# Attention into a squared-ReLU feed-forward on one core: wider key chunks, the last one shared by two pairs of heads

## The chip, the core and the metric

The kernel runs on one core of one Trainium2 chip. A core has TensorE (matrix products, from weights that are loaded first, into PSUM), VectorE and ScalarE (element by element, from and to PSUM and SBUF), GpSimd, SyncE, and 16 DMA engines that all queues share. The engines run side by side, each through its own instructions in order, and wait for one another by semaphores. The metric is the time of one execution on the device in microseconds, the median of several runs. The profile is of one execution.

## The reference, cut to what matters

```python
# q, k, v: (8 batches, 12 heads, 448 positions, 64), fp32
scores = scale * np.matmul(q, k.transpose(0, 1, 3, 2))
m = np.max(scores, axis=-1, keepdims=True)
e = np.exp(scores - m)
attn = e / (np.sum(e, axis=-1, keepdims=True) + np.exp(-m) + 1e-09)
x = np.matmul(attn, v)            # heads side by side: (3584, 768)
h = x @ w_in                      # (768, 2048)
r = np.maximum(h, 0.0)
out = (r * r) @ w_out             # (2048, 768)
```

Without the subtraction of `m`, the weights are exp(s) / (sum of exp(s) + 1), and this is what the kernel computes.

## The kernel before

A *unit* is a pair of heads with a range of queries. Batch 0 has two rounds of six units (0 to 5 with queries 0 to 191, 6 to 11 with the other 256); every later batch has one round with all 448 queries, and units 12 to 17 are batch 1. The 448 keys of a head are cut into four chunks of 112, the keys with the same remainder by 4. A chunk's scores have its keys on the partitions and both heads' queries in the columns. ScalarE turns them into exps in `et`; the exps are the moving operand of `values`, and their sum over the chunks (`es`, made on VectorE) goes through a product with a constant column, which gives the row sums. In the batches 0 to 2, q and k are transposed on TensorE and copied by VectorE. The products with `w_in` (tiles in `ins`) and `w_out` (in `outs`) fill TensorE between the steps of the attention, in portions (`drain`, `rows`). A yield of a tile is one product; in the mode COLS2 each product is issued as two of 64 columns.

```python
RUN = 4
P = S // RUN            # 112
ON_PE = (0, 1, 2)
# ... pools: e_pool 4 buffers, es_pool 2, s_psum 2, x_psum 1, m_psum 3, v_pool 2 ...

def load_v(b, p0, p1):
    hs = slice(2 * p0, 2 * p1)
    if b not in vns:
        vns[b] = v_pool.tile([P, H, RUN, D], FP16, name="vn")
    nc.gpsimd.dma_start(out=vns[b][:, hs], in_=v_r[b, :, hs])

# ... load_natural: q by SyncE's and k by ScalarE's queue (pairs 0 to 2 of batch 0, fp32, into
# whole["q"] and whole["k"], two buffers of e_pool), the rest by GpSimd with a cast to fp16 ...

def transposes(b, pr):
    tp = mp_tile(FP16)
    for i, name in enumerate("qk"):
        for s in range(RUN):
            for h in range(2):
                nc.tensor.transpose(tp[64 * h:64 * h + 64, i, P * s:P * s + P],
                                    naturals[name, b, pr][:, h, s, :], ident[0:P, 0:P])
    if b not in qks:
        qks[b] = qk_pool.tile([128, 3, COLS], FP16, name="qk")
    parts = (0, S // 2, S) if b == 0 and pr < 3 else (0, S)
    for x, y in zip(parts, parts[1:]):
        nc.vector.tensor_copy(qks[b][:, 0:2, pr * S + x:pr * S + y], tp[:, :, x:y])

def scores(u, et, c, only=(0, 1)):
    b, pr, q0, n = u
    qk = qks[b]
    two = [] if n == S else s_psum.tile([P, 2, 512], FP32, name="sp")
    for kk in [2 * c + x for x in only]:
        sp = s_psum.tile([P, 2, 512], FP32, name="sp") if n == S else two
        if b in ON_PE:
            o = 0 if n == S else kk % 2 * n
            for h in range(2):
                r = slice(64 * h, 64 * h + 64)
                x = pr * S
                nc.tensor.matmul(sp[:, h, o:o + n], qk[r, 1, x + P * kk:x + P * kk + P],
                                 qk[r, 0, x + q0:x + q0 + n], start=True, stop=True)
        # ... batches 3 to 7, from transposed loads ...
        if n == S:
            exp(chunk(et, u, c, kk).rearrange("p (o x) -> p o x", o=2), sp[:, :, 0:S])
    if n < S:
        exp(et[:, 0:RUN * 2 * n].rearrange("p (c h x) -> p c h x", c=2, h=2)[:, c], two[:, :, 0:2 * n])

def add_chunks(u, et, es, half, step):
    n = u[3]
    if n == S:
        e = et.rearrange("p (k x) -> p k x", k=RUN)
        if step < 2:
            nc.vector.tensor_add((es, half[:, 0:2 * S])[step], e[:, 2 * step], e[:, 2 * step + 1])
        else:
            nc.vector.tensor_add(es, es, half[:, 0:2 * S])
    elif step == 1:
        nc.vector.tensor_add(half[:, 0:4 * n], et[:, 0:4 * n], et[:, 4 * n:8 * n])
    elif step == 2:
        f = half[:, 0:4 * n].rearrange("p (h j n) -> p h j n", h=2, j=2)
        nc.vector.tensor_add(es[:, 0:2 * n].rearrange("p (h n) -> p h n", h=2), f[:, :, 0, :], f[:, :, 1, :])

def values(u, et, xp, o=0):
    b, pr, _, n = u
    for kk in range(RUN):
        for h in range(2):
            nc.tensor.matmul(xp[64 * h:64 * h + 64, o:o + n], vns[b][:, 2 * pr + h, kk, :],
                             of_head(chunk(et, u, kk // 2, kk), u, h), start=(kk == 0), stop=(kk == RUN - 1))

def row_sums(us, sums):

    n = us[0][3]
    m = n * len(us)
    zp = mp_tile()
    for j, (u, parts) in enumerate(zip(us, sums)):
        for x, es in enumerate(parts):
            total = es[:, 0:2 * n]
            if n < S:
                total = total.rearrange("p (h n) -> p h n", h=2)
            for h in range(2):
                nc.tensor.matmul(zp[64 * h:64 * h + 64, j * n:(j + 1) * n], ones, of_head(total, u, h),
                                 start=(x == 0), stop=(x == len(parts) - 1))
    rcp = z_pool.tile([128, 512], FP32, name="rcp")
    nc.scalar.activation(out=rcp[:, 0:m], in_=zp[:, 0:m], func=AF.Ln, bias=one_b)
    nc.scalar.activation(out=rcp[:, 0:m], in_=rcp[:, 0:m], func=AF.Exp, scale=-1.0)
    return rcp

# ... front of the program ...
for pr in range(3):
    load_natural(0, pr, pr + 1)
nc.scalar.preload_act_table_set("natural_log_exp_and_others")
ident = consts.tile([128, 128], FP16)
make_identity(nc, ident)
load_v(0, 0, 3)
load_natural(0, 3, 4)
load_natural(0, 4, 6)
load_v(0, 3, 6)
for i in range(4):
    load_win(i, 8)
load_natural(1, 0, 3)
for i in range(4, 8):
    load_win(i, 8)
load_natural(1, 3, 6)
load_v(1, 0, 6)

FIRST = 192
units = [(0, pr, 0, FIRST) for pr in range(NPAIR)] + [(0, pr, FIRST, S - FIRST) for pr in range(NPAIR)]
units += [(b, pr, 0, S) for b in range(1, B) for pr in range(NPAIR)]
NU = len(units)

transpose_at = {pr - 1: [(0, pr)] for pr in range(1, NPAIR)}
for i, at in ((10, (1, 0)), (11, (1, 1)), (11, (1, 2)), (13, (1, 3)), (14, (1, 4)), (15, (1, 5)), (16, (2, 0)),
              (17, (2, 1)), (17, (2, 2))):
    transpose_at.setdefault(i, []).append(at)

# ...
keep_warm(9)
cast(0, 0)
transposes(0, 0)
keep_warm(1)
cast(0, 1)

for i in range(NPAIR):
    u, et, es, half = begin(i)
    mode[0] = COLS2
    scores(u, et, 0)
    if i < 2:
        scores(u, et, 1)
    if i in (3, 5):
        rcp = sums_of(i - 3)
    for at in transpose_at.get(i, ()):
        transposes(*at)
    if i == 0:
        cast(0, 2)
        keep_warm(1)
    if i:
        sums(i - 1)
    if i > 1:
        scores(u, et, 1)
    if i in (2, 4):
        xp = x_psum.tile([128, 512], FP32, name="xp")
    if i in (2, 3, 4):
        values_of(i - 2, xp)
    if i == 4:
        values_of(3, xp)
    if i in (3, 5):
        normalise(units[i - 3:i - 1], xp, rcp)
    if i in (1, 3, 5):
        keep_warm(1 + i // 5)

for i in range(NPAIR, 2 * NPAIR):
    u, et, es, half = begin(i)
    two = units[i - 2:i] if i % 2 == 0 else None
    if i % 2 or i == NPAIR:
        xp = x_psum.tile([128, 512], FP32, name="xp")
    mode[0] = COLS2
    scores(u, et, 0)
    if i == NPAIR:
        sums(i - 1)
        values_of(i - 2, xp)
        values_of(i - 1, xp)
        rcp = sums_of(i - 2)
        normalise(two, xp, rcp)
        scores(u, et, 1)
        queue(0, FIRST)
        share[0] = left() / (NPAIR + 4)
    else:
        for at in transpose_at.get(i, ()):
            transposes(*at)
        drain(16 * FIRST / 2.4 if i == NPAIR + 1 else share[0] * 0.45)
        scores(u, et, 1)
        values_of(i - 1, xp)
        if two:
            rcp = sums_of(i - 2)
        drain(share[0] * 0.3)
    add_chunks(u, et, es, half, 1)
    if two and i > NPAIR:
        normalise(two, xp, rcp)
    add_chunks(u, et, es, half, 2)
    if i > NPAIR:
        drain(share[0] * 0.25)
    if i == NPAIR + 5:
        load_natural(2, 0, 3)
        for n0 in (0, HALF):
            for j in range(2):
                load_wout(n0, j, 2)

for i in range(2 * NPAIR, 3 * NPAIR):
    u, et, es, half = begin(i)
    prev = units[i - 1]
    first = i == 2 * NPAIR
    if not first:
        xp = x_psum.tile([128, 512], FP32, name="xp")
    mode[0] = COLS2
    scores(u, et, 0)
    for at in transpose_at.get(i, ()):
        transposes(*at)
    if i == 2 * NPAIR + 3:
        load_natural(2, 3, 6)
        load_v(2, 0, 6)
        stage(3)
    drain(share[0] * (1.2 if first else 0.45))
    scores(u, et, 1)
    if first:
        done = units[i - 2:i]
        values(prev, ets.pop(i - 1), xp, prev[3])
        rcp = row_sums(done, (ess.pop(i - 2)[0:1], ess.pop(i - 1)[0:1]))
    else:
        done = [prev]
        rcp = row_sums(done, (ess.pop(i - 1)[0:1],))
        values(prev, ets.pop(i - 1), xp)
    drain(share[0] * 0.15)
    for step in range(3):
        add_chunks(u, et, es, half, step)
        drain(share[0] * (0.15, 0.1, 0.15)[step])
    if i == 3 * NPAIR - 1:
        run(ins, len(ins))
        rcps[i] = row_sums([u], (ess.pop(i)[0:1],))
    normalise(done, xp, rcp)
    if first:
        queue(FIRST, S - FIRST)
        share[0] = left() / (NPAIR - 0.2)
```

From unit 18 on the units come in groups of three, with `outs` beside the scores and `ins` after them, and `begin` takes `et` from `e_pool` or, for two units of every other group, from the buffers `nn0` and `nn1` that held q and k of batches 1 and 2.

The softmax here doesn't subtract the row's maximum and nothing guards it: scores larger than these inputs give would overflow.

## Time and profile before

| | |
|---|---|
| Time, median of 3 runs (lowest to highest) | 412.77 us (412.49 to 413.12) |
| Span of the profiled execution | 410.6 us |
| TensorE busy | 401.0 us, 98% |
| VectorE busy | 289.8 us, 71% |
| ScalarE busy | 234.4 us, 57% |
| GpSimd busy | 36.3 us, 9% |
| Granted TensorE clock, mean | 0.999 |
| DMA, whole span | 45.58 MB, mean 111 GB/s |

How to read the profile. Busy times count the time in which an engine has an instruction in work. TensorE's instructions are pipelined and their ends are modelled, so 98% is not TensorE at its peak. A line of a group of instructions names the line of the kernel, the engine, the operation, the tile that is written and those that are read, partitions x elements and type, and the count; then the busy time in us, the mean of one in ns, and the idle time of the engine ahead of them with what ended it. Where 448 elements for each of two heads are one instruction, the line says 896. In the chain that ended last, each piece is what released the next one, or what stood before it on the same engine. In the busy times by stretch, an instruction counts to where it falls, and the average over the whole program says nothing of a stretch of its own kind.

### The profile page before, as it was taken

How to read it: one execution, taken by the hardware profiler on the slowest of the kernel's cores; microseconds unless marked ns; L12 is line 12 of the kernel's file. 1: busy time of each engine (PE TensorE's matmuls, PEld its weight loads, DVE VectorE, ACT ScalarE, POOL GpSimd, SP SyncE). 2: the span in 40 equal slices, each digit the busy share in tenths (PEclk: the TensorE clock that was granted, in tenths of full speed). 3: DMA queues.
4: the chain of work that ended last, by engine and by line, in shares of the span. 5: the costliest groups of instructions: out<-in, count | busy, mean ns of one | idle time of the engine just before them, and what ended most of it. 6: DMA issues, size and time to landing. Idle time of an engine off the chain costs nothing.

```text
span 410.6 us, 10685 instructions
## 1 busy us (share of the span) xinstructions
PE 401.0 (98%) x4715; PEld 259.0 (63%) x4715; DVE 289.8 (71%) x554; ACT 234.4 (57%) x312; POOL 36.3 (9%) x58
## 2 busy tenths in 40 slices
PE   7899998999999999999999999999999999999997
PEld 3577676755576666666566666667566665555664
DVE  3778896978976787777876788867876789186000
ACT  5998997667393745559383755739464663100111
POOL 7524030020000200001000030001000000000000
PEclk9999999999999999999999999999999999999999
DMA  9999999689114891499304992297102010010222
GB/s 203 197 198 197 203 202 219 127 132 219 60 42 107 135 219 25 98 183 182 100 2 114 168 179 64 77 188 124 41 2 69 11 41 2 38 40 0 78 77 78
DMA packets 75823, 45.58 MB, mean 111 GB/s; under 512 B 42560, under 2 KB 72000, under 8 KB 75456
## 3 DMA queue, kind: packets, MB, share of 16 engines
q0 software_dynamic: 28848, 22.16, 35.6%
q1 hardware_dynamic: 46208, 22.05, 23.1%
q8 instruction: 37, 0.61, 0.6%
q10 hardware_dynamic: 720, 0.69, 0.5%
q14 instruction: 10, 0.08, 0.1%
HBM read 45.69 MB, written 17.93 MB: 155 GB/s over the span
## 4 chain that ended last, share of the span: by engine, by line
PE 89%; ACT 4%; DVE 4%; DMA 1%; issue 1%
PE mp L286 24%; PE mp L352 17%; PE mp L288 11%; PE xp L286 8%; PE sp L201 6%; PE xp L352 5%; PE mp L236 5%; PE xp L288 3%; PE xp L236 3%; PE sp L189 3%; ACT et L169 3%; PE mp L250 2%; PE mp L158 1%; DMA et<-in_k_dram 1%; DVE qk L164 1%; ACT rcp L253 1%
## 5 line engine op out<-in xcount | busy, mean ns | idle before, releaser
L169 ACT ACTIVATE et<-sp 112x896 f16<-112x896 f32 (+2 forms) x144 | 125.2, 915 | 40.7 <-PE sp L201 30.6
L352 PE MATMUL mp<-wout,gs 64*128 64x384 f16 x896 | 115.2, 322 | 0.0
L286 PEld LDWEIGHTS <-win 128*64 128x64 f16 x1536 | 83.9, 110 | 45.6 <-issue 1.5
L286 PE MATMUL mp<-xt,win 128*64 128x448 f16 (+2 forms) x1200 | 107.0, 323 | 0.3 <-DVE qk L164 0.2
L293 DVE TENSOR_SCALAR rt<-mp 128x448 f16<-128x448 f32 (+2 forms) x96 | 59.7, 622 | 26.3 <-PE mp L286 13.8
L352 PEld LDWEIGHTS <-gs 64*128 64x128 f16 x1152 | 58.1, 94 | 21.1
L295 DVE TENSOR_TENSOR gs<-rt 128x448 f16<-128x448 f16 (+2 forms) x128 | 50.2, 392 | 4.4
L352 PE MATMUL xp<-wout,gs 64*128 64x384 f16 x256 | 53.1, 323 | 0.0
L253 ACT ACTIVATE rcp<-mp,one_b 128x448 f32<-128x448 f32 (+2 forms) x42 | 26.5, 630 | 41.9 <-PE mp L250 41.7
L361 ACT ACTIVATE ot<-mp 128x384 f32<-128x384 f32 (+1 forms) x16 | 7.6, 477 | 64.5 <-PE mp L288 48.2
L201 PE MATMUL sp<-qk 64*112 64x224 f16 x480 | 43.1, 258 | 0.0
L169 ACT ACTIVATE nn<-sp 112x896 f16<-112x896 f32 x48 | 41.7, 917 | 1.6
L201 PEld LDWEIGHTS <-qk 64*112 64x112 f16 x480 | 30.6, 128 | 14.2 <-issue 3.6
L286 PE MATMUL xp<-xt,win 128*64 128x448 f16 x336 | 36.5, 352 | 0.0
L288 PEld LDWEIGHTS <-gs 128*128 128x128 f16 x256 | 24.4, 98 | 15.1 <-issue 0.4
L236 PEld LDWEIGHTS <-vn 112*64 112x64 f16 x432 | 22.4, 109 | 15.4 <-issue 3.9
L288 PE MATMUL mp<-wout,gs 128*128 128x384 f16 (+1 forms) x192 | 30.3, 317 | 0.0
L214 DVE TENSOR_TENSOR es<-et 112x896 f16<-112x896 f16 x30 | 18.7, 623 | 15.8 <-ACT et L169 15.3
L254 ACT ACTIVATE rcp<-rcp 128x448 f32<-128x448 f32 (+2 forms) x48 | 27.7, 577 | 1.5
L189 PE MATMUL sp<-qk 64*112 64x448 f16 (+2 forms) x192 | 25.8, 320 | 1.4 <-ACT et L169 0.6
L216 DVE TENSOR_TENSOR es<-es,half 112x896 f16<-112x896 f16 x42 | 26.2, 623 | 1.0
L293 DVE TENSOR_SCALAR rt<-xp 128x448 f16<-128x448 f32 x32 | 19.9, 622 | 8.2 <-PE xp L286 6.7
(63 smaller groups left out, 340.0 us busy)
## 6 DMA issues: line engine op xcount, KB each, us to landing
vn<-in_v_dram POOLq DMA_DIRECT2D x7, 672.0 KB, 9.0
out_dram<-ot SPq DMA_DIRECT2D x9, 384.0 KB, 2.3
win<-in_moe_w_in_dram POOLq DMA_DIRECT2D x8, 384.0 KB, 14.2
wout<-in_moe_w_out_dram POOLq DMA_DIRECT2D x4, 768.0 KB, 18.0
stage_q<-in_q_dram POOLq DMA_DIRECT2D x4, 676.0 KB, 11.3
stage_k<-in_k_dram POOLq DMA_DIRECT2D x4, 676.0 KB, 14.7
out_dram<-ot SPq DMA_DIRECT2D x8, 288.0 KB, 9.0
out_dram<-ot SPq DMA_DIRECT2D x9, 192.0 KB, 2.7
```

Source lines behind the costliest of these rows:

```text
L169: nc.scalar.activation(out=out_, in_=in_, func=AF.Exp, scale=scale)
L189: nc.tensor.matmul(sp[:, h, o:o + n], qk[r, 1, x + P * kk:x + P * kk + P], qk[r, 0, x + q0:x + q0 + n], start=True, stop=True)
L201: nc.tensor.matmul(sp[:, odd, h * (S // 2):(h + 1) * (S // 2)], qk[r, which, kx:kx + 2 * P - 1:2], qk[r, 0, x:x + S // 2], start=True, sto ...
L216: nc.vector.tensor_add(es, es, half[:, 0:2 * S])
L236: nc.tensor.matmul(xp[64 * h:64 * h + 64, o:o + n], vns[b][:, 2 * pr + h, kk, :], of_head(chunk(et, u, kk // 2, kk), u, h), start=(kk == 0 ...
L253: nc.scalar.activation(out=rcp[:, 0:m], in_=zp[:, 0:m], func=AF.Ln, bias=one_b)
L254: nc.scalar.activation(out=rcp[:, 0:m], in_=rcp[:, 0:m], func=AF.Exp, scale=-1.0)
L286: nc.tensor.matmul(out_[x:x + 64], lhsT[:, x:x + 64], rhs, start=start, stop=stop)
L288: nc.tensor.matmul(out_, lhsT, rhs, start=start, stop=stop)
L293: nc.vector.tensor_scalar(out=rt[:, 0:m], in0=hp[:, 0:m], scalar1=0.0, scalar2=None, op0=ALU.max)
L295: nc.vector.tensor_mul(gs[:, f0:f0 + per, t0 % RING:t0 % RING + n], r, r)
L352: nc.tensor.matmul(o[:, 0:w], g[x:x + 64], wout[x:x + 64, fb, n0:n0 + w], start=(fb == 0), stop=(fb == NFFB - 1))
```

## The change

In batches 0 and 1 the keys are cut into three chunks of 128 (keys 0 to 383 by their remainder by 3) and one of 64 (keys 384 to 447). The 64-key chunks of two neighbouring pairs of heads share one tile of 128 partitions, the even pair above, the odd one below. Two pairs then need seven chunks of exps instead of eight, and all 128 partitions are in use. One of the two units, its owner, does the shared chunk: the second of the two in the first round, the first in the later rounds. What is meant to become shorter is ScalarE's share.

Other parts follow from it:

- *k in natural order.* The transposes leave the keys sorted by their remainder by 4, so the copy of k out of PSUM puts them into natural order, with a stepped read. It is an instruction apart from q's copy. For the first pair, q and k have PSUM tiles of their own, and ScalarE copies q.
- *v.* It is loaded in two parts, 384 rows of each head in runs of three rows, and the last 64 rows of each head in four transfers of single rows. For batch 0 three of these four go by SyncE's queue and one by ScalarE's, uncast, into unused columns of the buffers `whole`, and VectorE casts them. In the fourth chunk the rows of the other pair are zeros, set at the start.
- *Sums.* `es` adds three chunks instead of four, by two additions without `half`. The shared chunk enters the row sums by a second pair of products per unit, with weights that are zero in the other pair's half (`halves`).
- *Order.* In the first round the values of units 0 and 1 are taken together at unit 3. In batch 1's round one pair is transposed per unit, 12 to 17, where unit 12 had none and unit 17 two. The loads of batch 2's second half come one unit earlier. From unit 18 on every third unit takes `et` from `nn0` or `nn1`.

The diff, cut to its core ("..." marks a cut):

```diff
+    WIDE = (0, 1)
+    RW = 3
+    SW = 128 * RW
...
-        nc.gpsimd.dma_start(out=vns[b][:, hs], in_=v_r[b, :, hs])
+            vns[b] = v_pool.tile([128, H, RUN, D], FP16, name="vn")
+        if b in WIDE:
+            nc.gpsimd.dma_start(out=vns[b][:, hs, 0:RW], in_=v[b, hs, 0:SW].rearrange("h (p t) d -> p h t d", t=RW))
+        else:
+            nc.gpsimd.dma_start(out=vns[b][0:P, hs], in_=v_r[b, :, hs])
+
+    def last_v(b, j, h):
+
+        return (vns[b].rearrange("p (r j h) t d -> p j h r t d", j=2, h=2)[64 * j:64 * j + 64, j, h, :, RW, :],
+                v[b].rearrange("(r j h) s d -> j h s r d", j=2, h=2)[j, h, SW:S])
+
+    def load_last_v(b):
+        for j in range(2):
+            for h in range(2):
+                to, src = last_v(b, j, h)
+                if b:
+                    nc.gpsimd.dma_start(out=to, in_=src)
+                else:
+                    (nc.scalar if (j, h) == (0, 1) else nc.sync).dma_start(out=raw_v(j, h), in_=src)
+
...
+    def cast_last_v():
+        for j in range(2):
+            for h in range(2):
+                nc.vector.tensor_copy(last_v(0, j, h)[0], raw_v(j, h))
+
+    def clear_v(b):
+
+        vns[b] = v_pool.tile([128, H, RUN, D], FP16, name="vn")
+        rows = vns[b].rearrange("p (r j h) t d -> p j r h t d", j=2, h=2)
+        for j in range(2):
+            nc.vector.memset(rows[64 - 64 * j:128 - 64 * j, j, :, :, RW, :], 0.0)
 
...
+        tps = [mp_tile(FP16)] * 2
+        if b == 0 and pr == 0:
+            tps = [mp_tile(FP16), tps[0]]
+        tp = tps[1]
         for i, name in enumerate("qk"):
             for s in range(RUN):
                 for h in range(2):
-                    nc.tensor.transpose(tp[64 * h:64 * h + 64, i, P * s:P * s + P],
+                    nc.tensor.transpose(tps[i][64 * h:64 * h + 64, i, P * s:P * s + P],
                                         naturals[name, b, pr][:, h, s, :], ident[0:P, 0:P])
         if b not in qks:
             qks[b] = qk_pool.tile([128, 3, COLS], FP16, name="qk")
-        parts = (0, S // 2, S) if b == 0 and pr < 3 else (0, S)
-        for x, y in zip(parts, parts[1:]):
-            nc.vector.tensor_copy(qks[b][:, 0:2, pr * S + x:pr * S + y], tp[:, :, x:y])
+        o = qks[b][:, :, pr * S:(pr + 1) * S]
+        if b not in WIDE:
+            nc.vector.tensor_copy(o[:, 0:2], tp[:, :, 0:S])
+            return
+
+        nc.vector.tensor_copy(o[:, 1].rearrange("p (n s) -> p n s", s=RUN), tp[:, 1, 0:S].rearrange("p (s n) -> p n s", s=RUN))
+        if b == 0 and pr == 0:
+            nc.scalar.activation(out=o[:, 0], in_=tps[0][:, 0, 0:S], func=AF.Copy)
+        elif b == 0 and pr < 3:
+            for x, y in ((0, FIRST), (FIRST, S)):
+                nc.vector.tensor_copy(o[:, 0, x:y], tp[:, 0, x:y])
+        else:
+            nc.vector.tensor_copy(o[:, 0], tp[:, 0, 0:S])
 
 
 
...
+    def wide_scores(u, et, c, last):
+        b, pr, q0, n = u
+        qk = qks[b]
+        kks = (0, 1) if c == 0 else (2, 3) if last else (2,)
+        two = [] if n == S else s_psum.tile([128, 2, 512], FP32, name="sp")
+        for kk in kks:
+            sp = s_psum.tile([128, 2, 512], FP32, name="sp") if n == S else two
+            o = 0 if n == S else kk % 2 * n
+            pairs = (pr,) if kk < RW else (pr // 2 * 2, pr // 2 * 2 + 1)
+            for h in range(2):
+                r = slice(64 * h, 64 * h + 64)
+                for j, of in enumerate(pairs):
+                    x = of * S
+                    keys = slice(x + kk, x + SW, RW) if kk < RW else slice(x + SW, x + S)
+                    to = slice(0, 128) if kk < RW else slice(64 * j, 64 * j + 64)
+                    nc.tensor.matmul(sp[to, h, o:o + n], qk[r, 1, keys], qk[r, 0, x + q0:x + q0 + n],
+                                     start=True, stop=True)
+            if n == S:
+                exp(chunk(et, u, c, kk).rearrange("p (o x) -> p o x", o=2), sp[:, :, 0:S])
+        if n < S:
+            m = len(kks) * n
+            exp(et[:, 0:RUN * 2 * n].rearrange("p (c h x) -> p c h x", c=2, h=2)[:, c, :, 0:m], two[:, :, 0:m])
 
...
+            if u[0] in WIDE:
+                nc.vector.tensor_add(es, (e[:, 0], es)[step], e[:, 1 + step])
+            elif step < 2:
+                nc.vector.tensor_add((es, half)[step][0:P], e[0:P, 2 * step], e[0:P, 2 * step + 1])
             else:
-                nc.vector.tensor_add(es, es, half[:, 0:2 * S])
-        elif step == 1:
-            nc.vector.tensor_add(half[:, 0:4 * n], et[:, 0:4 * n], et[:, 4 * n:8 * n])
-        elif step == 2:
-            f = half[:, 0:4 * n].rearrange("p (h j n) -> p h j n", h=2, j=2)
-            nc.vector.tensor_add(es[:, 0:2 * n].rearrange("p (h n) -> p h n", h=2), f[:, :, 0, :], f[:, :, 1, :])
+                nc.vector.tensor_add(es[0:P], es[0:P], half[0:P])
+        else:
+            e = et[:, 0:RUN * 2 * n].rearrange("p (c h j n) -> p c h j n", c=2, h=2, j=2)
+            s = es[:, 0:2 * n].rearrange("p (h n) -> p h n", h=2)
+            nc.vector.tensor_add(s, (e[:, 0, :, 0], s)[step], (e[:, 0, :, 1], e[:, 1, :, 0])[step])
 
...
+            parts = [(ones, total), (halves[:, u[1] % 2], last_chunk(i))] if u[0] in WIDE else [(ones[0:P], total[0:P])]
+            for x, (w, part) in enumerate(parts):
                 for h in range(2):
...
+    for b in WIDE:
+        clear_v(b)
...
+    load_last_v(0)
...
+    load_last_v(1)
...
-    for i, at in ((10, (1, 0)), (11, (1, 1)), (11, (1, 2)), (13, (1, 3)), (14, (1, 4)), (15, (1, 5)), (16, (2, 0)),
-                  (17, (2, 1)), (17, (2, 2))):
+    for i, at in ((10, (1, 0)), (11, (1, 1)), (11, (1, 2)), (12, (1, 3)), (13, (1, 4)), (14, (1, 5)), (15, (2, 0)),
+                  (16, (2, 1)), (17, (2, 2))):
...
+        if i >= 3 * NPAIR and i % 3 == 2:
+            ets[i] = nat.tile([128, RUN * 2 * S], FP16, name=f"nn{i // 3 % 2}")
+        else:
+            ets[i] = e_pool.tile([128, RUN * 2 * S], FP16, name="et")
...
+    def owns(i):
+
+        return i % 2 == (i < NPAIR) and units[i][0] in WIDE
+
+    def last_chunk(i):
+        return chunk(lasts[i if owns(i) else i ^ 1], units[i], 1, RW)
+
+    def visit(i, c):
+        wide_scores(units[i], ets[i], c, owns(i))
+
...
+        if i == 2:
+            cast_last_v()
         if i > 1:
-            scores(u, et, 1)
-        if i in (2, 4):
+            visit(i, 1)
+        if i in (3, 4):
             xp = x_psum.tile([128, 512], FP32, name="xp")
-        if i in (2, 3, 4):
-            values_of(i - 2, xp)
-        if i == 4:
-            values_of(3, xp)
+        if i in (3, 4):
+            values_of(2 * i - 6, xp)
+            values_of(2 * i - 5, xp)
...
+        if not first:
+            for at in transpose_at.get(i, ()):
+                transposes(*at)
+        if i == 2 * NPAIR + 2:
             load_natural(2, 3, 6)
             load_v(2, 0, 6)
             stage(3)
...
+            transposes(1, 3)
```

## Prediction

> **What bounds the kernel now.** I read the totals and slices of the page first, then busy time by stretch. I cut the span where the program changes its work: A (0 to 18.25 us, queries 0 to 191 of batch 0), B (to 36.3, the other 256 queries), C (to 67.5, batch 1), D (the rest). Columns are start and end, length, then busy us (and instructions) of TensorE, weight loads, VectorE, ScalarE and GpSimd, the granted clock, the DMA share and GB/s:
>
> ```profile
> 0.00:18.25 18.25, 15.61 (x203) 8.45 (x204) 10.23 (x27) 12.92 (x19) 12.40 (x21) 1.00 1.18 200
> 18.25:36.30 18.05, 16.33 (x296) 12.34 (x295) 14.10 (x29) 15.81 (x20) 5.46 (x7) 1.00 1.45 197
> 36.30:67.50 31.20, 29.04 (x458) 20.98 (x456) 27.86 (x53) 26.96 (x36) 6.40 (x9) 1.00 1.40 208
> 67.50:410.60 343.10, 340.00 (x3762) 217.20 (x3760) 237.62 (x447) 178.74 (x239) 12.05 (x22) 1.00 0.45 93
> ```
>
> D is TensorE alone (340.0 of 343.1) and the change hardly enters it. So only the first 67.5 us can move. There the idle TensorE time is 2.64 us in A, 1.72 in B and 2.16 in C. ScalarE is at 88% in B and 86% in C, VectorE at 89% in C: three engines close together, which says that freeing one alone brings little. The chain that ended last shows a unit of C (columns: start, length, what):
>
> ```profile
> 44.02 1.20 PE mp L286 x22
> 45.22 0.52 PE sp L189 x4
> 45.74 0.52 PE mp L158 x16
> 46.26 0.98 PE mp L286 x18
> 47.24 0.53 PE sp L189 x4
> 47.76 0.31 PE mp L250 x2
> 48.08 0.76 PE xp L236 x8
> ```
>
> That is TensorE without a gap, 4.82 us; ScalarE has only 4 x 0.80 + 1.2 = 4.4 us in it. In the next unit VectorE takes over (rt, gs, two adds, xt, copy, 49.31 to 52.74) and TensorE's row sums wait for its copy, so the unit takes 5.1 us. A, however, is a chain of hand-overs: transpose, VectorE copy, scores, exp:
>
> ```profile
> 7.05 0.60 PE mp L158 x16
> 7.68 0.40 DVE qk L164
> 8.13 0.67 PE sp L189 x8
> 8.80 0.70 PE mp L158 x16
> 9.52 0.69 DVE qk L164 x2
> ```
>
> The durations that I use, from the groups by shape in the first 70 us:
>
> ```profile
> L169 ACT ACTIVATE et<-sp 112x1024 f16<-112x1024 f32 x12 | 11.8, 1016 | 1.0 <-PE sp L189 0.7
> L169 ACT ACTIVATE et<-sp 112x768 f16<-112x768 f32 x12 | 9.4, 806 | 1.0 <-PE sp L189 0.9
> L164 DVE COPY qk<-mp 128x896 f16<-128x896 f16 x12 | 7.3, 619 | 1.0 <-PE mp L158 1.0
> L262 DVE TENSOR_TENSOR xt<-xp,rcp 128x448 f16<-128x448 f32 x5 | 3.1, 618 | 0.0
> L164 DVE COPY qk<-mp 128x448 f16<-128x448 f16 x6 | 2.1, 386 | 2.2 <-PE mp L158 2.2
> ```
>
> [...] doubling the fp16 copy from 448 to 896 elements costs 233 ns, 0.52 ns each, while an fp32 operation on 448 takes 618 ns. [...] two row sums of 448 columns together occupy 0.19 us in the chain, but a block of four score matmuls 0.52, not 0.38. [...] No small packets are in the trace; [...] the engines are at 9 tenths for the first 60 us.
>
> **The change, part by part.**
> *Exps.* An exp costs (1016 - 806)/256 = 0.82 ns per element. Every second unit of batch 0 loses 384 elements in the first half (0.315 us) and 512 in the second (0.42), and every second unit of batch 1 one exp of 896 (four in a row take 3.32, so 0.80 apart). Sum: 3 x 0.315 + 3 x 0.42 + 3 x 0.80 = 4.6 us less on ScalarE, less about 0.55 for the first pair's q copy, which moves there: 4.1 us.
> *Adds.* Per unit of batch 0: 551 + 358 ns become 2 x 358, and 689 + 422 become 2 x 422: 0.19 and 0.27 less, six of each, 2.8 us. Batch 1 drops one add of 0.62 six times: 3.7 us.
> *Copies.* k is now read with step 112 from PSUM. [...] 0.62 us for 448, and q apart 0.386. So 0.619 becomes 1.01 (+0.39) in pairs 3 to 5 and in all six of batch 1; pairs 1 and 2 go from 0.77 to 0.62 + 0.25 + 0.29 = 1.16 (+0.39, the small ones at 154 ns + 0.52 per element); pair 0 from 0.77 to 0.62. Sum +4.1. Four casts of 192 elements of v, about 0.25 each: +1.0. VectorE's net: -2.8 - 3.7 + 4.1 + 1.0 = -1.4 us, with the additions early and the savings late.
> *TensorE.* The row sum of each of 18 units gets a second pair of matmuls: 6 x (0.19 + 0.11 + 0.08, by columns) = +2.3 us. The shared chunk's four 64x64 products may run four at a time, -1.1 at best. Net +1.2.
> *DMA.* The same bytes; 768 B and 256 B packets in place of 1 KB, for v of batches 0 and 1.
>
> **On the path.**
> A. Pair 0's scores start when k's copy ends, 0.2 us later. Pair 1's need 0.62 + 0.25 of copies where 0.39 was enough (+0.4), pair 2 again (+0.3), and the casts of v (about 0.85 with their starts) now lie ahead of pair 4's copy, where VectorE had only 0.76 idle. Following the in-order queues unit by unit, unit 5's second exp starts about 1.0 us later than now, though ScalarE has less to do: +1.0.
> B. Here ScalarE does run back to back (five exps in 4.87 us). 3 x 0.42 = 1.26 is saved; some of it sits before waits for TensorE (0.47 and 0.26 us at units 10 and 11) and is lost; the cheaper adds give 0.3 and the second of two adjacent copies costs VectorE 0.3. -1.0, so C starts about where it does now.
> C. Unit 13 has three exps, and its fourth score pair no longer waits for ScalarE (0.41 us now): -0.6. Units 13 to 17 stay bound by TensorE: second row sums +0.19 each, scores about even: +0.7 after what VectorE's lighter load returns. Unit 17 now transposes one pair, not two: it drops the 0.22 wait and half a us of transposes, which goes into unit 12, where TensorE waits anyway, and the 1.13 wait for the last sum shrinks by one add: -1.2. Sum -1.1.
> D. 0. Total +1.0 - 1.0 - 1.1 = -1.1, so 412.77 - 1.1 = 411.7 us.
>
> **Rivals.**
> 1. ScalarE's whole 4.1 us arrives (408.7). For: 86 to 88% busy in B and C. Against: the gap-free TensorE chain above; B and C together have only 3.9 us of TensorE idle, and 1.2 of new work goes in.
> 2. The last rows of v come too late. Batch 1's v is issued at 25.48 and lands 16.4 us later, at 41.9; its first use is at 43.27. Four more transfers of 256 B packets queue behind it[...]; the small byte count (a seventh of v) and the 1.4 us of slack against. If it lands at 44.5, TensorE stands for about 2 us: 413.7.
> 3. A costs more than I think: copies and casts on VectorE sit directly between transposes and exps, and the pairs loaded for batch 0 arrive just in time (the last k at 4.42 + 8.2 = 12.6, its transposes begin at 12.60). A at +2.5 gives 413.2.
> 4. The end of C loses its waits altogether and the shared products overlap four at a time: 410.
>
> **Range and chances.** Errors of A (±1), the v transfer (0 to +2) and C (±1.2) are largely independent: 409.4 to 414.0. Two per cent is 8.3 us. All the TensorE idle before D is 6.5 us, so faster by that is nearly excluded (0.02); slower would need several late transfers (0.02).
>
> **What would show it.** Right: exp instances of 128 partitions, three fewer of 896; strided copies near 0.62 us; A about 1 us longer; C about 1 us shorter with TensorE gap-free in its units; D unchanged. Wrong: strided copies at 0.39 (A then no longer, total near 410); a wait of values for v at unit 13 (413 and up); unit times in C near 4.4, which would mean that TensorE was not the limit (near 409); or D longer, from its other order of exp buffers.

## The result, and the profile after

| | before | after |
|---|---|---|
| Time, median of 4 runs each (lowest to highest) | 412.69 us (412.49 to 413.12) | 417.75 us (416.85 to 417.95) |
| Ratio, with its 95% interval | | 1.0117 (1.0099 to 1.0134) |
| Span of the profiled execution | 410.6 us | 416.2 us |
| Granted TensorE clock, mean | 0.999 | 0.992 |

The change costs 5.1 us; predicted was a gain of 1.1. The prediction's stretches, cut in the changed kernel at the same events (A ends where the last exps of the first 192 queries of batch 0 begin, B where the first exp of batch 1 begins, C where the first score of batch 2 begins), show where. Busy time by stretch, changed kernel, columns as in the prediction:

```profile
0.00:24.41 24.41, 17.97 (x211) 9.73 (x211) 13.27 (x42) 12.45 (x19) 14.50 (x24) 0.86 1.27 199
24.41:42.61 18.20, 16.58 (x312) 12.29 (x308) 13.05 (x31) 14.66 (x20) 6.33 (x9) 1.00 1.43 182
42.61:72.86 30.25, 29.38 (x474) 20.99 (x473) 25.64 (x51) 24.76 (x33) 6.17 (x9) 1.00 1.34 207
72.86:416.20 343.34, 339.93 (x3762) 216.84 (x3760) 237.23 (x447) 178.75 (x239) 12.07 (x22) 1.00 0.45 91
```

A grew from 18.25 to 24.41 us, and its clock fell to 0.86. B went from 18.05 to 18.20, C from 31.22 to 30.25 (with batch 2's first score at 67.52 before), and D stayed (343.08 and 343.34). So the loss is in A, where TensorE has 6.4 us idle instead of 2.6.

Two lines of the changed kernel's list of waits (engine and tile that waited, engine and tile waited for; us in total, times, longest) name it:

```profile
ACT et L218 <- DVE vn L110: 4.4, 1, 4.4
PE sp L242 <- ACT et L218: 3.6, 2, 3.3
```

ScalarE waits once, 4.4 us, for a *cast of v*, which an exp does not read. The next lines are VectorE's in time order, changed kernel (start, length, what; in brackets the idle time before it and what ended it), and in the second fence ScalarE's:

```profile
12.35 0.62 DVE L206 COPY qk<-mp 128x448 f16<-128x448 f16 x1 [0.68 <-PE mp L197]
12.89 0.38 DVE L213 COPY qk<-mp 128x448 f16<-128x448 f16 x1
...
13.64 0.36 DVE L289 TENSOR_TENSOR es<-es,et 128x384 f16<-128x384 f16 x1
13.91 1.24 DVE L110 CAST vn<-et 64x192 f16<-64x192 f32 x4
```

```profile
9.05 1.51 ACT L218 ACTIVATE et<-sp 128x768 f16<-128x768 f32 x2 [0.64 <-PE sp L242]
14.97 1.19 ACT L218 ACTIVATE et<-sp 128x768 f16<-128x768 f32 x2 [4.41 <-DVE vn L110]
```

The casts read from `et`: the raw rows of v lie at the end of `whole["q"]` and `whole["k"]`, which are two of the four buffers of the pool for exps. Units 0 and 1 take the other two, so unit 2 gets the buffer of `whole["q"]`. The third cast is the last reader of `whole["q"]`, the fourth of `whole["k"]`, and unit 2's first exp begins at 14.97, before the fourth cast ends at 15.15. The exps of unit 2 write the first 3072 bytes of each partition, and the raw rows begin at byte 6144: the buffer is handed on when all its readers are done, whichever bytes they read (the wait is 4.41 us here). The casts stand in VectorE's queue behind the copies for pair 3 and both adds of unit 1. Before, unit 2's exp began at 10.38; now at 14.97. Then TensorE stands for 3.3 us, having no free score buffer.

And then TensorE runs at half clock. Busy time by stretches of 2.5 us, changed kernel (the clock is the third number from the end), then the 3.41 us ahead of the fall, and below the kernel before from 10 to 20 us:

```profile
12.50:15.00 2.50, 0.00 (x1) 0.10 (x1) 2.37 (x8) 0.03 (x1) 1.68 (x3) 0.73 1.54 197
15.00:17.50 2.50, 1.66 (x26) 1.36 (x27) 0.15 (x1) 2.24 (x4) 1.17 (x2) 0.50 1.46 194
17.50:20.00 2.50, 2.50 (x31) 1.64 (x27) 1.65 (x5) 1.57 (x3) 0.82 (x2) 0.50 1.45 197
20.00:22.50 2.50, 2.46 (x43) 1.44 (x42) 1.73 (x4) 1.20 (x2) 0.97 (x2) 0.91 1.46 197
```

```profile
10.24:13.65 3.41, 1.25 (x22) 0.81 (x23) 2.52 (x9) 0.32 (x1) 2.77 (x4) 1.00 1.48 192
```

```profile
10.00:20.00 10.00, 8.73 (x145) 5.67 (x146) 7.99 (x18) 9.16 (x14) 5.65 (x8) 1.00 1.45 197
```

The clock is 0.50 from 15 to 20 us, and was 1.00 before. 0.73 over the first stretch means half clock from 13.65 us on, 0.91 over the last means until 20.45: 6.8 us in all. The clock falls only 1.2 us after TensorE's last product (which ends at 12.50), with two thirds of the wait of 3.3 us still to come, and in the 3.41 us ahead of the fall, half as long as the fall lasts, TensorE was busy 1.25 us. So the long wait alone does not explain the first fall; experiments 5 to 10 come back to this.

The sizes on which the prediction built its sum, changed kernel, groups by shape in the first 70 us:

```profile
L206 DVE COPY qk<-mp 128x448 f16<-128x448 f16 x12 | 7.4, 620 | 6.7 <-PE mp L197 6.7
L218 ACT ACTIVATE et<-sp 128x768 f16<-128x768 f32 x9 | 7.2, 808 | 8.0 <-DVE vn L110 4.4 <-PE sp L242 3.4 <-ACT et L218 0.3
```

The stepped copy of k takes 620 ns; the plain one of q took 0.38 us in VectorE's lines above. An exp over 128 partitions takes as long as one over 112 (808 against 806 ns). A unit of C is gap-free on TensorE; its instructions in time order, changed kernel:

```profile
58.64 0.38 PE L325 MATMUL mp<-es,ones 128*64 128x448 f16 x2
58.85 0.35 PE L325 MATMUL mp<-et,halves 128*64 128x448 f16 x2
59.04 0.92 PE L307 MATMUL xp<-et,vn 128*64 128x448 f16 x8
59.80 1.37 PE L361 MATMUL mp<-xt,win 128*64 128x256 f16 x22
61.10 0.56 PE L242 MATMUL sp<-qk 64*128 64x448 f16 x4
61.59 0.58 PE L197 MATMUL mp<-ident,nn 112*64 112x112 f16 x16
62.00 1.15 PE L361 MATMUL mp<-xt,win 128*64 128x256 f16 x18
63.09 0.68 PE L242 MATMUL sp<-qk 64*128 64x448 f16 x6
```

The second pair of row-sum products (`halves`) begins 0.21 us after the first and is 0.19 us ahead of the values. The six score products at 63.09 (a pair, and four of the shared chunk) take 0.68 us, where a pair alone takes 0.37 in the unit before: the four of 64 keys, each 0.37 us long in the trace, add 0.31 us in all, no more than one pair of 128 keys.

### The profile page after: what moved, and what is told of

It reads as the page before. It is cut to its first block, busy times and chain, and to the rows that moved or that the text cites. A ratio compares the mean times of both kernels' runs of the same rounds, so it can differ in the third digit from the quotient of the medians.

```text
span 416.2 us, 10789 instructions
## 1 busy us (share of the span) xinstructions
PE 403.9 (97%) x4751; PEld 259.8 (62%) x4751; DVE 289.2 (69%) x569; ACT 230.6 (55%) x310; POOL 39.1 (9%) x62
## 4 chain that ended last, share of the span: by engine, by line
PE 87%; DMA 9%; DVE 1%; POOL 1%; ACT 1%; issue 0%; POOLq 0%; DVEq 0%
PE mp L361 23%; PE mp L427 17%; PE mp L363 10%; PE xp L361 8%; PE sp L271 6%; PE xp L427 5%; PE mp L307 5%; DMA vn<-in_v_dram 5%; DMA win<-in_moe_w_in_dram 4%; PE xp L363 3%; PE xp L307 3%; PE mp L325 2%; PE sp L242 1%; PE sp L259 1%; PE mp L197 1%; POOL nn L135 1%
## 5 line engine op out<-in xcount | busy, mean ns | idle before, releaser
L218 ACT ACTIVATE et<-sp 112x896 f16<-112x896 f32 (+5 forms) x141 | 121.1, 900 | 50.4 <-PE sp L271 30.6
L307 PEld LDWEIGHTS <-vn 112*64 112x64 f16 (+1 forms) x432 | 22.9, 112 | 15.3 <-issue 2.6
L283 DVE TENSOR_TENSOR es<-et 112x896 f16<-112x896 f16 x24 | 14.9, 622 | 15.5 <-ACT et L218 15.5
L285 DVE TENSOR_TENSOR es<-es,half 112x896 f16<-112x896 f16 x36 | 22.4, 623 | 0.8
L434 DVE TENSOR_SCALAR ot<-mp 128x384 f32<-128x384 f32 x28 | 15.6, 557 | 9.6 <-PE mp L427 6.1
```

What stands on the lines that cost most here:

```text
L218: nc.scalar.activation(out=out_, in_=in_, func=AF.Exp, scale=scale)
L285: nc.vector.tensor_add(es[0:P], es[0:P], half[0:P])
L307: nc.tensor.matmul(xp[64 * h:64 * h + 64, o:o + n], vns[b][r, 2 * pr + h, kk, :], of_head(e, u, h), start=(kk == 0), stop=(kk == RUN - 1))
L434: nc.vector.tensor_scalar(out=ot[:, n0:n0 + w], in0=op[:, 0:w], scalar1=OUT_SCALE, scalar2=None, op0=ALU.mult)
```

## The experiments

All times are medians; the kernel before, run beside each set on the same chip, took 412.59, 412.51 and 412.52 us in the three sets. Theory: (1) the buffer's release and (2) the halved clock that follows are most of the loss; (3) stepped copies and casts on A's chain of hand-overs are the rest. Rivals: the halved clock is only a by-product that costs little; v comes late; C gives back less than it should.

**1. The raw rows of v in a buffer of their own** (`own_raw`). All else as in the changed kernel.

```diff
+    raw_pool = ctx.enter_context(tc.tile_pool(name="raw", bufs=1))
+    raw = raw_pool.tile([128, 2, NPAIR // 2, D], FP32, name="raw")
 ...
     def raw_v(j, h):
-        x = NPAIR // 2 * 512
-        return whole["qk"[h]][64 * j:64 * j + 64, x:x + NPAIR // 2 * D].rearrange(...)
+        return raw[64 * j:64 * j + 64, h]
```

> The changed kernel with one edit: the uncast last rows of v get a buffer of their own instead of unused columns of the q and k buffers. Theory (the exp of unit 2 waits for VectorE's casts because its buffer is the one they read): the 4.4 us wait of ScalarE goes, the first exp of unit 2 starts at 11 to 12 us instead of 14.97, the clock stays at 1.0 between 10 and 20 us, and the time falls from 417.8 to about 412.3 us. Rival, VectorE's added copies and casts alone make the first round longer: the exp starts early but unit 6's first exp still comes at 23 us or later, time about 416. Rival, the four small transfers land late: the wait moves to the values of unit 3 behind casts that wait for a DMA, time about 415.

Measured: 414.49 us, ratio 1.0048 (1.003 to 1.0067). 3.3 of the 5.1 us are gone, with the same transfers and the same casts, so the late v is excluded as the cause of the wait. ScalarE's line for unit 2's exps in this version:

```profile
11.34 1.20 ACT L219 ACTIVATE et<-sp 128x768 f16<-128x768 f32 x2 [0.63 <-PE sp L243]
```

They wait for scores again, not for casts. (The chain of waits of the changed kernel had put this stretch down to the transfer of v, 10.61 us from 5.15 us on; here the transfer is the same and the wait is gone.) But the time is 2.2 us over the expected one, and its four executions lie 2 us apart (413.53 to 415.54), where those of the kernel before lie within 0.8 us. Both had to be explained.

**2. Idle products in the gap** (`warm_gap`). The changed kernel, with 14 products of zeros in the gap. The wait stays; only TensorE is kept at work.

```diff
         if i > 1:
             visit(i, 1)
+        if i == 2:
+            keep_warm(14)
```

> The changed kernel with 14 idle products of 512 columns put behind unit 2's last scores, where TensorE stands for 3.3 us. They only keep it busy. Theory: the wait of 4.4 us stays, the granted clock in the slice from 10 to 20 us rises from 0.68 to nearly 1, and what the lower clock cost goes: TensorE ran the products of 15.8 to 20.3 us at about half speed, some 1.3 us on the path, so 416.5 us. Rival, the clock is the main loss: about 413. Rival, the clock cost nothing because TensorE was not the limit there: 417.8.

Measured: 415.54 us (415.44 to 415.66), ratio 1.0073 (1.0058 to 1.0088). The wait is still 4.0 us, the mean clock 0.999 to 1.000 in all four executions. So the halved clock cost about 417.75 - 415.54 = 2.2 us, more than the 1.3 expected, and is not a by-product. (The one execution of the changed kernel with a mean clock of 0.995, a single period of half clock, took 416.85. In the profiles, unit 2's exps also begin 0.5 us earlier here, at 14.50, since TensorE's transposes did not wait 0.45 us for k; so the clock's part may be smaller by as much.)

**3. The new order of transposes alone** (`order_only`), in the kernel before:

```diff
-    for i, at in (..., (13, (1, 3)), (14, (1, 4)), (15, (1, 5)), (16, (2, 0)), (17, (2, 1)), (17, (2, 2))):
+    for i, at in (..., (12, (1, 3)), (13, (1, 4)), (14, (1, 5)), (15, (2, 0)), (16, (2, 1)), (17, (2, 2))):
 ...
         if first:
+            transposes(1, 3)
             queue(FIRST, S - FIRST)
```

> The kernel before with only the new order: one pair transposed per unit from 12 to 17, and the loads of batch 2's second half one unit earlier. Theory of the prediction: unit 17 loses one of its two transposes and its waits, the work goes into unit 12 where TensorE waits anyway; about 1 us less, 411.7. Rival, VectorE is the limit in the units and takes the copy in either place: 412.7.

Measured: 412.34 us, ratio 0.9997 (0.9989 to 1.0006): no difference clear of noise. TensorE still waits for the last sum at the end of C; its line in this version, the same 1.13 us as before:

```profile
67.49 0.38 PE L250 MATMUL mp<-es,ones 112*64 112x448 f16 x2 [1.13 <-DVE es L216]
```

In the profile, unit 17's wait of 0.22 us for a copy is gone, but TensorE now waits 0.45 us in unit 12 ahead of the new transposes, and C is 30.97 us for 31.22. So the order is worth 0.25 us at most by these profiles, and the half us or more that the prediction gave to it is not there.

**4. Wide chunks in batch 1 alone** (`b1_only`). Batch 0 as before, batch 1 and the order as changed; no raw rows, no casts on VectorE.

```diff
-    WIDE = (0, 1)
+    WIDE = (1,)
```
(with the code of before for batch 0's scores, adds and copies)

> Wide chunks for batch 1 alone, batch 0 as in the kernel before, with the new order of transposes. Theory (all of the loss is in batch 0's first round, the round of batch 1 gains 1.0 us as the changed kernel's trace shows): 411.9. Rival, the stepped copies of batch 1's k on VectorE at units 10 and 11 and the later v take the gain back: 413.

Measured: 411.99 us (411.75 to 412.53, 12 runs), ratio 0.9987 (0.9978 to 0.9996). A gain of 0.6 us, and the fastest of all whole computations here. C's gain is real (30.24 us for 31.22 in the profile); B is 0.37 us longer than before, so the rival's stepped copies take a part of it back. Batch 0's wide chunks lose.

**5 to 8. What is left in batch 0.** Version 1 still lies 2.5 us over version 4. Four variants of version 1 take a suspect away each. `own_flat` copies k without a step (it leaves out the reordering of the keys):

```diff
-        nc.vector.tensor_copy(o[:, 1].rearrange("p (n s) -> p n s", s=RUN),
-                              tp[:, 1, 0:S].rearrange("p (s n) -> p n s", s=RUN))
+        nc.vector.tensor_copy(o[:, 1], tp[:, 1, 0:S])
```

> Raw last v in a buffer of its own, and k copied from PSUM without a step (this leaves out the reordering of the keys, so chunks of keys no longer match those of v; every instruction keeps its size). It asks where the 1.9 us are that remain over the kernel before at 414.5. Theory 'stepped copies': each of them lies between a transpose and the scores that wait for it, 0.62 us where an unstepped one takes about 0.39, for pairs 1 to 5 of batch 0 and for two pairs at the end of batch 0: 7 x 0.24 = 1.7 us less, so 412.9. Rival 'casts and second row sums': the copies lie beside other work, 414.3.

`own_nocast` leaves batch 0's last rows of v out, with zeros in their place:

```diff
-    load_last_v(0)
 ...
-        if i == 2:
-            cast_last_v()
```

> Raw last v in a buffer of its own, but batch 0's last v neither loaded nor cast (left out: 64 of 448 keys add no value in batch 0; zeros stand in their place). Theory 'casts': four of 0.34 us stand on VectorE ahead of the copies for pair 4 and push the chain of transposes, copies and exps back by 0.9 to 1.3 us: 413.4. Rival 'stepped copies': VectorE would have waited there for TensorE anyway, 414.3.

`own_both` has both edits.

> Both at once: k copied without a step, and batch 0's last v neither loaded nor cast. If the two costs add up they explain the 1.9 us: 411.8 to 412.3, first exp of batch 1 at 36.3 to 36.8 us. If TensorE's second row sums (0.38 us per pair of units) and its hand-overs set the length of batch 0, it stays at 413.3 or more.

`own_act` computes everything, with the casts on ScalarE behind unit 2's exps:

```diff
-                nc.vector.tensor_copy(last_v(0, j, h)[0], raw_v(j, h))
+                nc.scalar.activation(out=last_v(0, j, h)[0], in_=raw_v(j, h), func=AF.Copy)
```

> The whole computation: raw last v in a buffer of its own, and its four casts moved from VectorE to ScalarE, behind the exps of pair 2. Theory: ScalarE waits for TensorE in batch 0's first half anyway, so the casts cost little there: 413.7. Rival: the exps of pair 3 then start 1.4 us later and TensorE with them: 415.

Measured: 414.31, 414.17, 411.75 and 414.77 us; ratios 1.0043 (1.0028 to 1.0058), 1.0032 (1.0014 to 1.0051), 0.9978 (0.9969 to 0.9987) and 1.0056 (1.0041 to 1.0071). Read as medians this makes no sum: one edit gives 0.2, the other 0.3, both 2.7. For the single edits the rival's figure (414.3) was met, and with both the theory's (411.8); neither can be true of the same kernel. The single executions with their mean clocks resolve it:

| version | clock 0.999 to 1.000 | 0.995 or 0.996 | 0.992 |
|---|---|---|---|
| own_raw | 413.53 | 414.35, 414.62 | 415.54 |
| own_flat | none | 413.72, 413.94 | 414.69, 414.99 |
| own_nocast | 412.35, 412.88, 412.92 | 414.02, 414.32 | 414.93, 414.94, 415.13 |
| own_both | 411.23 to 412.42 (all 12) | none | none |
| own_act | none | 414.29, 414.54 | 415.00, 415.64 |

The mean clock comes in steps of 0.004. Over a span of 412 us a step is about 1.7 us of lost full clock, or one period of about 3.4 us at half clock: that of `own_flat` lasts from 12.65 to 16.06 us by the clocks of its stretches, half as long as the 6.8 us of the changed kernel. The first such period costs `own_nocast` 1.3 us (414.17 against 412.88), the second 0.8. Within a column the edits do count: own_flat 0.65 to 0.7 where 1.6 was expected, own_nocast 0.3 to 0.65 where 1.1 was, and both together 1.8 against the one execution of own_raw at full clock. So each edit holds at about half its expected size; together they are worth more than the sum of the two, which stays open. The rest of the 2.7 is that `own_both` never loses the clock. own_act lies within about 0.2 us of own_raw in each column that both have: four casts of v cost nearly the same on ScalarE as on VectorE, and its expected 0.8 us didn't come.

What the profile shows when it happens, in `own_flat`: TensorE's three waits ahead of the fall, then the busy time and clock by stretch:

```profile
10.28 0.35 PE L243 MATMUL sp<-qk 64*128 64x192 f16 x4 [0.33 <-ACT et L219]
...
11.27 0.39 PE L198 MATMUL mp<-ident,nn 112*64 112x112 f16 x8 [0.33 <-DMA nn<-in_k_dram]
...
12.45 0.37 PE L243 MATMUL sp<-qk 64*128 64x192 f16 x4 [0.59 <-DVE qk L214]
```

```profile
9.00:12.50 3.50, 2.24 (x42) 1.27 (x43) 2.35 (x9) 2.57 (x4) 2.42 (x3) 1.00 1.42 191
12.50:16.00 3.50, 3.50 (x48) 2.76 (x50) 3.02 (x10) 2.72 (x4) 2.24 (x3) 0.52 1.52 195
```

No wait of TensorE is over 0.6 us, yet the clock halves: it was busy 2.24 of 3.5 us by the trace. Here many short waits were enough. It is not always so: the profiled execution of `own_raw` was as thinly filled and kept its clock (mean 1.000):

```profile
9.39:12.80 3.41, 2.06 (x43) 1.23 (x39) 2.79 (x9) 2.52 (x4) 2.54 (x4) 1.00 1.42 191
```

**9. The same version, kept at work** (`own_warm`): version 1 with five more idle products in A.

```diff
-        if i in (1, 3, 5):
-            keep_warm(1 + i // 5)
+        if i in (1, 2, 3, 5):
+            keep_warm((3, 3, 1, 0, 2)[i - 1])
```

> Raw last v in a buffer of its own, and five more idle products on TensorE where it waits in batch 0's first half (two after pair 1, three after pair 2). Theory: of the 1.9 us that this version lacked to the kernel before, about 1 us is the halved clock that comes for 3.3 us in some of its executions; with TensorE kept busy the mean clock is 0.999 to 1.000 in every execution, and the time 413.2, near the fastest execution without them (413.5). Rival: the spread has another cause, and the idle products only stand in the way: 414.5 to 415, still spread over 2 us.

Measured: 413.36 us (413.31 to 413.70, 11 runs), ratio 1.0022 (1.0013 to 1.0031), every clock 0.999 or 1.000. As expected to 0.2 us: the spread is gone, and 1.1 us of version 1's median with it. The stretch where the clock fell in `own_flat`, here:

```profile
9.00:12.50 3.50, 3.37 (x50) 1.68 (x48) 2.88 (x9) 2.71 (x4) 2.42 (x3) 1.00 1.41 190
```

**10. The kernel before, without its single idle products in A** (`before_cold`):

```diff
         if i == 0:
             cast(0, 2)
-            keep_warm(1)
 ...
-        if i in (1, 3, 5):
-            keep_warm(1 + i // 5)
```

> The kernel before, with the five single idle products of batch 0's first half left out (nine and one at the start stay). Theory: TensorE's activity between 5 and 20 us is what holds the clock; with some 1.1 us of it gone the clock is halved in some executions, mean clock 0.992 or 0.996, and those take 413.8 to 415. Rival: [...] 412.5, clock 0.999 to 1.000 always.

Measured: 413.12 us median of 20 runs, from 412.25 to 417.44, ratio 1.0019 (1.0006 to 1.0031). Eight executions at 0.999 or 1.000 have a median of 412.4, eleven at 0.996 of 413.5, one at 0.979 took 417.44. The profiled execution kept its clock, so where it falls in the others is not shown. The theory holds in a kernel without any part of the change: without these products in A the clock fell in 12 of 20 executions, with them in none of the 30 run beside (0.999 or 1.000 in each). The size was less than expected (1.1 us, mostly a single period).

**11 and 12. What bounds batch 1.** From version 4: `b1_norow` leaves the second pair of row-sum products out (so the last 64 keys of batch 1 are missing from the row sums); `b1_add` lets VectorE add the shared chunk's rows instead, the whole computation:

```diff
-            parts = [(ones, total), (halves[:, u[1] % 2], last_chunk(i))] if u[0] in WIDE else [...]
+            parts = [(ones, total)] if u[0] in WIDE else [...]
 ... (b1_add alone, after the last of a unit's adds)
+                    nc.vector.tensor_add(es[r], es[r], last_chunk(i)[r])     # r: 64 of the 128 partitions
```

> Wide chunks in batch 1 alone, and there the second pair of row-sum products left out (this leaves the last 64 keys of batch 1 out of the row sums; all else is computed). Theory: TensorE sets the length of the units of batch 1, so six times 0.19 us come off in full: 410.85 against 411.99. Rival: VectorE or ScalarE takes over in these units: 411.7.

> Wide chunks in batch 1 alone, the whole computation: in place of the second pair of row-sum products, VectorE adds the shared chunk's 64 rows into the sum over the other chunks (one more add of 0.62 us per unit). Theory: TensorE loses 6 x 0.19 us and VectorE, which the dropped third add had relieved, has room: 411.0. Rival: VectorE becomes the bound, as in the kernel before, and row sums wait for the last add: 412.2 or more.

Measured: `b1_norow` 410.82 us, ratio 0.9961 (0.9946 to 0.9976); that is 1.17 us under version 4, and 6 x 0.19 = 1.14. TensorE bounds the units of C to the last tenth. `b1_add` 414.29 us, ratio 1.0041 (1.0026 to 1.0056): missed by 3.3 us. The same work on VectorE is no substitute. One group of `b1_add` in C (36 to 70 us), TensorE's row sums, with the idle time ahead of them:

```profile
L337 PE MATMUL mp<-es,ones 128*64 128x448 f16 x12 | 2.3, 370 | 3.8 <-DVE qk L205 1.5 <-DVE qk L215 1.2 <-DVE es L292 1.1
L292 DVE TENSOR_TENSOR es<-es,et 64x896 f16<-64x896 f16 x6 | 3.7, 620 | 0.4
```

They wait 3.8 us for VectorE (0.7 in version 4, without these adds), 2.7 of it for the copies. An add on 64 partitions takes 620 ns, as on 128 (618 and 623 ns in the same version).

## Why the prediction was wrong, step by step

With the clock held until the last step, the 5.1 us come apart (the two middle versions differ also in where the idle products stand):

| step | from, to | us |
|---|---|---|
| batch 1's wide chunks, with the new order | before 412.6, b1_only 412.0 | -0.6 |
| batch 0's wide chunks, casts and copies, clock held | b1_only 412.0, own_warm 413.4 | +1.4 |
| exps wait for the casts, clock held | own_warm 413.4, warm_gap 415.5 | +2.2 |
| clock halved in two periods | warm_gap 415.5, after 417.7 | +2.2 |

**A, predicted +1.0, was +6.2.** The step that failed is "the casts of v (about 0.85 with their starts) now lie ahead of pair 4's copy". They were counted as VectorE's time on the path of the copies (they took 1.24 us, not 1.0), and not as readers of a buffer that unit 2's exps need. The kernel shows it: `raw_v` points into `whole`, and `whole` is made with `e_pool.tile`. Rival 3 had the stretch right ("A costs more than I think") but for copies and casts between transposes and exps, and at 2.5. The clock was taken as 1.00 throughout, from the trace of before, though that kernel has idle products in A for just this purpose.

Without wait and clock, the step holds in kind: in `own_warm`, unit 5's last exps begin at 19.80 against 18.25, so +1.55 for +1.0. A single profile is no closer than half a us here: in `order_only`, whose A has the same instructions as before, they begin at 18.78. With unstepped copies and no casts (`own_both`) they begin at 18.89, so the two edits account for about 0.9. What else there is wasn't taken apart.

**B, predicted -1.0, was +0.15.** The step "3 x 0.42 = 1.26 is saved; some of it sits before waits for TensorE and is lost" failed in its size: all of it was lost. ScalarE's busy time did fall (15.81 to 14.66), and its waits grew: ahead of batch 1's first exp it waits for scores, 0.63 us before (first line) and 1.45 in the changed kernel:

```profile
36.30 3.35 ACT L169 ACTIVATE et<-sp 112x896 f16<-112x896 f32 x4 [0.63 <-PE sp L189]
42.61 2.54 ACT L218 ACTIVATE et<-sp 128x896 f16<-128x896 f32 x3 [1.45 <-PE sp L242]
```

In `own_both` that wait is 1.21, so the step in the copies of batch 1's first pairs explains 0.24 of it. TensorE's products just ahead of these scores wait 0.50 us for those copies in `own_warm` (the changed kernel's trace puts a wait of 0.49 in the same place down to a transfer of v), and not at all before. In `b1_only`, which has these copies and batch 0's chunks as before, B is 18.42: the copies cost 0.37, and batch 0's wide chunks gave back only 0.22. Why they gave no more stays open.

**C, predicted -1.1, was -0.97.** Right in sum, wrong in a part. Right: TensorE gap-free in its units, second row sums 0.19 each (`b1_norow` confirms their cost in full), and the wait for the last sum, 1.13 before, is 0.47 now that an add is gone. Wrong: the share given to the order of transposes, which alone moves at most 0.25 us (experiment 3). That the sum came out all the same is partly luck: the score products, which the prediction took as about even, became shorter, since four of 64 keys add 0.31 us where one pair takes 0.37. (The line of the prediction's unit gives 0.31 us for a pair of row sums; the 0.19 that it used is the distance between starts, and that is what the second pair cost.)

The last sum of C in the changed kernel, to be read against the line of 1.13 in experiment 3:

```profile
72.36 0.38 PE L325 MATMUL mp<-es,ones 128*64 128x448 f16 x2 [0.47 <-DVE es L281]
```

**D, predicted 0, was +0.26.** Right: executions of the kernel before lie up to 0.8 us apart as a whole.

**The rivals.** ScalarE's whole gain (408.7) did not come. v was never late: in C no value product waits for it; the 2 us set aside for it were the author's estimate, which no trace of before had shown. The reading "no small packets are in the trace" was wrong: of the 75,823 packets of the kernel before, 42,560 are under 512 B, though only 490 of the 20,332 in the first 60 us. The smaller terms of the working were good: 0.62 us for a stepped copy (the author's estimate, taken over from an fp32 operation on 448 elements at 618 ns; 620 ns measured), exps no longer with 128 partitions than with 112 (808 and 806 ns), four products of 64 x 64 in the time of a pair (0.31 and 0.37 us). The three errors, taken as independent, give 410.1 to 414.2 and not 409.4 to 414.0; either range failed because the errors were those of known instructions, and none stood for a wait that the change itself makes.

## What to carry to other kernels

Before raw data is parked in a spare corner of a pool's buffer, list who gets that buffer next: the next owner waits for the last reader of any part of it (4.41 us in the changed kernel), and that reader stands behind whatever its engine has in its queue. Where TensorE works in a chain of hand-overs, watch the granted clock of each execution and not the median time alone: two edits that each seemed worth 0.2 or 0.3 us by the medians were worth 2.7 together, of which 1.8 are the edits at full clock and the rest is that with both of them no execution lost the clock. A saving on an engine that isn't the bound of its stretch (here 4 us of exps) is worth what the bound gains, and an addition to the bound (0.19 us per row sum) is paid in full.

## What the runs showed of the hardware that was not expected

- The clock fell to half after 3.41 us in which TensorE was busy 2.15 us (`own_flat`, 9.24 to 12.65 us) and never waited more than 0.6. In the changed kernel TensorE was busy 1.25 us in the 3.41 us ahead of the fall, so it was not idle throughout there either. From 9.39 to 12.80 us TensorE was busy 2.15 us in `own_flat` and 2.02 in `own_act` (both at half clock from the end of this stretch on), and 2.06 in `own_raw`, whose profiled execution kept its clock and whose other three did not; it was busy 2.39 us in `own_both`, 2.91 in the kernel before and 3.20 in `own_warm`, which kept it in every execution of the experiments. This rests on one profile for each version, with transposes counted as busy.
- Whether it falls differs between executions of one program: in `before_cold` in 12 of 20, in `own_nocast` in 5 of 8. What decides it in one execution was not shown.
- A fall costs less than the clock it takes: one period of half clock is about 1.7 us of full clock and cost 0.8 to 1.3 us (`own_nocast`, `before_cold`). That the rest lay beside waits for other engines is argued, not shown.
